# Moving a cluster step between two matmul stages of an attention kernel, and loading the first q by contiguous rows

## The chip, the core and the metric

The kernel runs on one core of one Trainium2 chip. The metric is the device time of one execution in microseconds (us), the median of the runs of a kernel. The core has five engines that run their own instruction queues side by side and meet only through semaphores: TensorE (PE in the profile, its weight loads PEld), VectorE (DVE), ScalarE (ACT), GpSimd (POOL) and SyncE (SP, here only an issuer of DMAs).

## What is computed

A routing attention is followed by a mixture of experts. Each query and each key is assigned to the most similar of 16 cluster centroids of its head, and a query attends only to keys of its own cluster.

```python
# B, H, S, D = 4, 8, 768, 64; 16 clusters
q_assign = np.argmax(np.einsum('bhsd,hcd->bhsc', q_n, c_n), axis=-1)
k_assign = np.argmax(np.einsum('bhsd,hcd->bhsc', k_n, c_n), axis=-1)
mask = q_assign[:, :, :, None] == k_assign[:, :, None, :]
scores = np.where(mask, scale * np.matmul(q, k.transpose(0, 1, 3, 2)), -1e9)
attn = softmax(scores)
attn_out = np.matmul(attn, v)
# x = attn_out as (3072, 512): each token goes to the best of 8 experts (512 -> 1024 -> 512, relu)
```

## The kernel before

The attention works through 16 pairs of heads (NG = 16; a pair is two heads of one batch, and fills the 128 partitions). The order of instructions on each engine is the order of the program. A pair is a **turn**: twelve units of scores, then the jobs of the part "mid", then twelve units of weighted values, then the jobs of the part "end".

```python
for n in range(-4, NTURN + 2):
    for i, x in enumerate(range(n * NB, (n + 1) * NB)):     # NB = 12
        if 0 <= x < NU:
            score(x)
        run(n, i)
    run(n, mid)
    for i, x in enumerate(range(n * NB, (n + 1) * NB)):
        if 0 <= x < NU:
            attend(x)
        run(n, NB + i)
    run(n, end)
```

One unit of scores: four fp32 matmuls in two halves of the array's rows and two bf16 ones that add the cluster mask (`ohT`), an exponential on ScalarE, and a sum over key blocks on VectorE. The first block of a half has no sum of its own, so twelve units make ten sums.

```python
def score(u):
    ps = ps_s.tile([P, 2, 512], F32, name="sps")            # 3 buffers
    # ... matmul(ps, lhsT=qk[g], rhs=qk[g]) x2, matmul(ps, lhsT=ohT[g], rhs=ohT[g]) x2
    A[u] = ap.tile([P, 2, HS], F32, name="A")
    nc.scalar.activation(A[u], ps[:, :, 0:HS], AF.Exp, scale=D**-0.5)      # line 1005
    if g == NG - 2 and u % UG >= 3:                         # UG = 12
        later_sums.append((u, A[u]))
    else:
        add_up(u, A[u])                                     # DVE: lines 1019 and 1023
```

The cluster step of a pair makes `ohT` for its scores: similarities on TensorE, the maximum and its place on VectorE, one product on GpSimd, a transposition, and eight copies on ScalarE.

```python
def similar(g):
    ps = ps_o.tile([P, 512], F32, name="O") if g == 1 else wide()[:, 0, :]   # wide(): one of the 3 "sps"
    # ... 4 matmuls, each in its own quarter of the array's columns (line 914)
    sims[g] = asg.tile([P, HS], F32, name="sim")
    nc.vector.transpose(sims[g], ps[:, 0:HS])               # line 921

def assign(g):
    nc.vector.tensor_reduce(mx, sim, axis=AX, op=ALU.max)                    # line 930
    nc.vector.tensor_tensor(sim, sim, mx..., op=ALU.is_ge)                   # line 931
    (nc.gpsimd if g > 1 else nc.vector).tensor_tensor(sim, sim, first_c..., op=ALU.mult)   # line 932

def assign2(g):
    nc.vector.tensor_reduce(top, rank, axis=AX, op=ALU.max)                  # line 939
    nc.vector.tensor_tensor(oh, rank, top..., op=ALU.is_equal)               # line 941
    nc.vector.transpose(sims[g], oh)                        # "ohs", line 946

def put_by_scalar(g):
    # 4 times: copy (line 960) and activation (line 961) from ohs into ohT[g]
```

`weigh` sums the weights (12 fp32 matmuls, line 1060, also in quarters of the array's columns) and its result is transposed on VectorE (line 1068). `turn_blocks` transposes q and k of a pair on VectorE (line 899, two instructions). `finish` copies the output of a half on ScalarE (line 1046), `keep` transposes it on VectorE (line 1089) and stores it by DMAs from GpSimd. The jobs are placed so:

```python
for f in (similar, assign, assign2):
    at(0, 4, f, 1)
for g in range(NG):
    at(g, end, finish, g, 0)
    at(g, end, finish, g, 1)
    if g + 2 < NG:
        at(g, mid, turn_blocks, g + 2)
        at(g, end, similar, g + 2)
        at(g, end, assign, g + 2)
    if g < NG - 1:
        at(g, end, keep, g, 0, S)
        at(g + 1, mid, weigh, g)
        at(g, mid, put_by_scalar, g + 1)
    if g + 2 < NG:
        at(g, end, assign2, g + 2)
```

So the cluster step of a pair runs at the end of the turn two before its own, and its copies into `ohT` run in the middle of the next turn. For the first pair alone q and k are transposed by TensorE instead of VectorE (`turn`), because they are loaded whole:

```python
(nc.scalar if g == 0 and name == "k" else nc.sync).dma_start(       # line 775
    out=t[:, :, a, :],
    in_=src[b, 2 * hp + a].rearrange("(j p) d -> p j d" if name == "q" else "(p j) d -> p j d", j=NQ),
)
```

Of the kernel before, what the change touches and what calls it, by code (L numbers as in the profile page):

```python
# [8 lines left out]
F32 = mybir.dt.float32  # L9
# [176 lines left out]
def kernel(  # L186
# [11 lines left out]
    nc = tc.nc  # L198
    B, H, S, D = q.shape
    C = centroids.shape[1]  # L200
    P = 128
    NQ = S // P
# [3 lines left out]
    NG = B * HP  # L206
# [27 lines left out]
    def fetch1(e, i):  # L234
        w1 = wpool.tile([P, DB, F], F32, name=f"w1_{i % 2}")
        nc.sync.dma_start(out=w1, in_=moe_w1[bass.ds(e, 1)].rearrange("e (a p) f -> p (e a) f", p=P))
        return w1
# [29 lines left out]
    ps_o = late.enter_context(tc.tile_pool(name="ps_o", bufs=2, space=PSUM))  # L267
# [3 lines left out]
    def apart(first, second):  # L271

        first, second = (getattr(i, "ins", i) for i in (first, second))
        tc.declare_no_dep(second, first, reason="other banks and other elements")


    def wide():
        return pools["s"].tile([P, 2, 512], F32, name="sps")
# [4 lines left out]
    def bank():  # L283

        return wide()[:, 0, :] if "attention" in pools else ps_o.tile([P, 512], F32, name="O")
# [450 lines left out]
    with ExitStack() as actx:  # L736
# [17 lines left out]
        def load_qk(g):  # L754
            b, hp = divmod(g, HP)
            for name, src in (("q", q), ("k", k)):
                t = rows[g, name] = ld.tile([P, NQ, 2, D], F32, name=name + "_in")
                for quad in range(4 if g else 0):


                    a, d0 = quad // 2, quad % 2 * 32
                    o = t[quad * 32 : (quad + 1) * 32].rearrange("p j a d -> p (j a d)")
                    if name == "q":
                        nc.sync.dma_start(  # L764
                            out=o.rearrange("p (b d) -> p b d", d=32),
                            in_=src[b, 2 * hp + a].rearrange("(b p) d -> p b d", p=32)[:, :, d0 : d0 + 32],
                        )
                    else:
                        nc.sync.dma_start(
                            out=o.rearrange("p (i m d) -> p i m d", m=4, d=32),  # L770
                            in_=src[b, 2 * hp + a].rearrange("(m p i) d -> p i m d", m=4, i=NQ)[:, :, :, d0 : d0 + 32],
                        )
                for a in range(0 if g else 2):

                    (nc.scalar if g == 0 and name == "k" else nc.sync).dma_start(
                        out=t[:, :, a, :],
                        in_=src[b, 2 * hp + a].rearrange("(j p) d -> p j d" if name == "q" else "(p j) d -> p j d", j=NQ),
                    )

        def load_v(g):  # L780
# [35 lines left out]
        ps = bank()  # L816
# [44 lines left out]
        def blocks():  # L861
            cps = bank()
            nc.tensor.transpose(cps[:, 0:P], cn.rearrange("p a d -> p (a d)"), ident)
            cview = cps[:, 0:P].rearrange("p (g a c) -> p g a c", a=2, c=C)
            for a in range(2):
                nc.vector.tensor_copy(cblk[a * D : (a + 1) * D, :, a, :], cview[a * D : (a + 1) * D, :, a, :])


        qk, sims, ohT = {}, {}, {}

        def turn(g, piece):

            if piece == 0:
                qk[g] = qkp.tile([P, 2, S], F32, name="qk")
            n = NQ - 4 if piece else 4
            ps = wide().rearrange("p a c -> p (a c)")
            for i in range(2 * n):
                w, j = divmod(i, n)
                if i == n and piece == 0:
                    blocks()  # L880
                nc.tensor.transpose(
                    ps[:, w * 512 + j * P : w * 512 + (j + 1) * P], rows[g, "qk"[w]][:, 4 * piece + j].rearrange("p a d -> p (a d)"), ident
                )
            if piece == 0:
                apart(
                    nc.vector.tensor_copy(qk[g][:, 0, 0:512], ps[:, 0:512]),
                    nc.scalar.copy(qk[g][:, 1, 0:512], ps[:, 512:1024]),
                )
            else:
                apart(*(  # L890
                    copy(qk[g][:, w, 512:S], ps[:, w * 512 : w * 512 + n * P])
                    for w, copy in enumerate((nc.vector.tensor_copy, nc.scalar.copy))
                ))

        def turn_blocks(g):

# [10 lines left out]

        def similar(g):


            ps = ps_o.tile([P, 512], F32, name="O") if g == 1 else wide()[:, 0, :]
            for t in range(4):
                w, half = divmod(t, 2)
                nc.tensor.matmul(  # L914
                    ps[t * 2 * C : (t + 1) * 2 * C, 0:HS], lhsT=cblk[:, g % HP].rearrange("p a c -> p (a c)"),
                    rhs=qk[g][:, w, half * HS : (half + 1) * HS], start=True, stop=True,
                )


            sims[g] = asg.tile([P, HS], F32, name="sim")  # L920
            nc.vector.transpose(sims[g], ps[:, 0:HS])
# [64 lines left out]
        A, T, O = {}, {}, {}  # L986
        XT = {}

        def where(u):
            g, r = divmod(u, 2 * NQ)  # L990
            return g, r // NQ, r % NQ

        def score(u):
            g, half, j = where(u)
            qs = slice(half * HS, (half + 1) * HS)
            ks = slice(j * P, (j + 1) * P)
            ps = ps_s.tile([P, 2, 512], F32, name="sps")
            for a in range(2):
                r = slice(a * D, (a + 1) * D)
                nc.tensor.matmul(ps[:, a, 0:HS], lhsT=qk[g][r, 1, ks], rhs=qk[g][r, 0, qs], start=True, stop=False)  # L1000
            for a in range(2):
                r = slice(a * D, (a + 1) * D)
                nc.tensor.matmul(ps[:, a, 0:HS], lhsT=ohT[g][r, 1, ks], rhs=ohT[g][r, 0, qs], start=False, stop=True)  # L1003
            A[u] = ap.tile([P, 2, HS], F32, name="A")
            nc.scalar.activation(A[u], ps[:, :, 0:HS], AF.Exp, scale=D**-0.5)  # L1005
            if g == NG - 2 and u % UG >= 3:
                later_sums.append((u, A[u]))
            else:
                add_up(u, A[u])
# [3 lines left out]
        def add_up(u, a_u):  # L1013
            g, half, j = where(u)
            if j == 0:
                last_a[0] = a_u
            elif j == 1:
                T[g, half] = tp_.tile([P, 2, HS], F32, name="T", bufs=4)
                nc.vector.scalar_tensor_tensor(
                    T[g, half], in0=last_a[0], scalar=1e-9 / P, in1=a_u, op0=ALU.add, op1=ALU.add  # L1020
                )
            else:
                nc.vector.tensor_tensor(T[g, half], T[g, half], a_u, op=ALU.add)  # L1023
# [110 lines left out]
        def at(n, part, f, *a):  # L1134
            jobs.setdefault((n, part), []).append((f, a))

        UG = 2 * NQ
# [3 lines left out]
        mid, end = "mid", "end"  # L1141
# [9 lines left out]
        at(0, 2, put_q, 0, 1)  # L1151
        at(-2, end, idle_of, 20)
        at(-1, end, turn_blocks, 1)
        for f in (similar, assign, assign2):
            at(0, 4, f, 1)
        for g in range(NG):
            at(g, end, finish, g, 0)
            at(g, end, finish, g, 1)
            if g + 2 < NG:
                at(g, mid, turn_blocks, g + 2)  # L1160
                at(g, end, similar, g + 2)
                at(g, end, assign, g + 2)
            if g < NG - 1:
                at(g, end, keep, g, 0, S)
                at(g + 1, mid, weigh, g)
                at(g, mid, put_by_scalar, g + 1)
            if g + 2 < NG:
                at(g, end, assign2, g + 2)
            if g % HP == HP - 1 and g < NG - 1:
                at(g + 1, mid, gate, g // HP)  # L1170
                at(g + 1, end, gate2, g // HP)
                at(g + 1, end, keep_pads, g // HP)
# [44 lines left out]
        n = NG - HP  # L1217
# [4 lines left out]
        at(n + 1, end, one_hots1, 1)  # L1222

        at(n + 2, UG + 3, tokens1)
        at(n + 2, UG + 3, sums_of_later, 2)
        at(n + 2, UG + 6, spread1)
        at(n + 2, UG + 6, gather1, 0)
        at(n + 2, UG + 6, sums_of_later, UG)
        at(n + 3, mid, gather1, 1)
        at(n + 3, mid, turn_rows1, 0)  # L1230

        n = NG
# [54 lines left out]
    with tc.tile_pool(name="sm", bufs=1) as sm:  # L1287
# [20 lines left out]
        for part in parts:  # L1308
            n, over = part["n"], part["over"]
# [95 lines left out]
    g = groups[0]  # L1405
# [61 lines left out]
    with tc.If(more > 0):  # L1467
        nx = nc.values_load(xe[0:1, NX : NX + 1], min_val=0, max_val=NX)
        general = nc.values_load(xe[0:1, NX + 1 : NX + 2], min_val=0, max_val=1)
        with tc.If(nx > XU):  # L1470
            with ExitStack() as ectx:
# [3 lines left out]
                with tc.For_i(XU, nx, 1) as i:  # L1475
# [5 lines left out]
                    g = dict(  # L1481
                        n=[P], rows=N, w=(fetch1(ex, 0), fetch2(ex, 0)), gi=lambda j, i: gi[:, i : i + 1],
                        si=lambda j: gi[:, 4:5], apart=False,
                    )
# [37 lines left out]
```

## Time and profile before

| what | value |
|---|---|
| median of 3 runs | 687.94 us (687.89 to 688.46) |
| span of the profiled execution | 687.2 us |
| TensorE busy | 674.8 us, 98% of the span |
| VectorE busy | 471.8 us, 69% |
| ScalarE busy | 310.6 us, 45% |
| GpSimd busy | 253.6 us, 37% |
| first exponential of pair 1, of pair 15 | 37.12 us, 313.73 us |
| last attention output copied | 331.6 us |

The first 332 us are the attention, the rest is the mixture of experts, which the change leaves as it is. The share of busy time is an average over both; the attention has to be read turn by turn. A busy TensorE is not TensorE at its peak, since the ends of pipelined matmuls are modelled. A timeline line gives start, length, engine, source line, operation, what it writes and reads, the number of instructions merged into it, and in brackets the idle time before it with what ended it.

### The profile page before, as it was taken

The page shows a single profiled execution, that of the slowest core. Times are in us where ns is not written, and L with a number is a line of the kernel's source. Part 1 is how long each engine was busy: PE and PEld are TensorE (multiplying, and loading weights), DVE is VectorE, ACT ScalarE, POOL GpSimd, SP SyncE. Part 2 cuts the span into 40 slices and gives each one's busy share as a digit, 9 for nine tenths or more (in the row PEclk, how much of TensorE's full clock was granted, in tenths as well). Part 3 has the DMA queues.
Part 4 walks back from the last instruction along what each step waited for, and adds up shares of the span by engine and source line. Part 5 has one row for each costly group of instructions (what it writes and reads, how often), then busy time and mean ns, then how long its engine had stood idle before and what let it go on. Part 6 is the DMA issues. An engine that isn't in the chain of part 4 may idle for free.

```text
span 687.2 us, 11979 instructions
## 1 busy us (share of the span) xinstructions
PE 674.8 (98%) x4603; PEld 440.1 (64%) x4603; DVE 471.8 (69%) x740; ACT 310.6 (45%) x470; POOL 253.6 (37%) x327
## 2 busy tenths in 40 slices
PE   8999999999999999999999999999999999999994
PEld 7444444445454444555656789878788787888761
DVE  6887888779887778889666549576755767564300
ACT  3887777778877777785111031211113111131100
POOL 5022222122222221257816774547352563412101
PEclk9999999999999999999999999999999999999997
DMA  7566864997759643421435349586676866668440
GB/s 144 90 93 93 154 140 86 152 150 153 117 74 195 98 68 38 49 48 33 68 125 176 119 135 371 198 291 207 233 268 212 306 195 236 244 230 300 161 140 20
DMA packets 149540, 106.71 MB, mean 155 GB/s; under 512 B 115554, under 2 KB 119650, under 8 KB 149475
## 3 DMA queue, kind: packets, MB, share of 16 engines
q1 hardware_dynamic: 135266, 77.41, 42.9%
q0 software_dynamic: 8640, 19.63, 13.0%
q10 hardware_dynamic: 5568, 8.83, 4.3%
q8 instruction: 38, 0.62, 0.4%
q14 instruction: 28, 0.22, 0.1%
HBM read 93.06 MB, written 13.30 MB: 155 GB/s over the span
## 4 chain that ended last, share of the span: by engine, by line
PE 74%; issue 14%; POOL 6%; DVE 2%; DMA 1%; SPq 1%; POOLq 0%; ACTq 0%; ACT 0%; DVEq 0%
PE sps L1000 17%; PE O L1038 17%; PE sps L321 9%; PE sps L498 8%; PE sps L386 7%; PE sps L520 5%; PE sps L1003 4%; POOL xg L292 3%; PE sps L1060 3%; POOL out_dram L341 2%; PE sps L914 2%; DMA k_in<-in_k_dram 1%; PE sps L357 1%; DVE T L1023 1%; SPq L764 0%
## 5 line engine op out<-in xcount | busy, mean ns | idle before, releaser
L1005 ACT ACTIVATE A<-sps 128x768 f32<-128x768 f32 x192 | 153.7, 810 | 22.3 <-PE sps L1003 21.0
L292 POOL DMA_INDIRECT xg<-x_rows,g_idx x104 | 120.4, 1158 | 115.5 <-DVE xgT L308 81.1
L1000 PE MATMUL sps<-qk 64*128 64x384 f32 x768 | 157.0, 487 | 0.0
L1023 DVE TENSOR_TENSOR T<-T,A 128x768 f32<-128x768 f32 x128 | 122.6, 958 | 13.1
L1038 PE MATMUL O<-A,v_in 128*64 128x384 f32 x768 | 127.8, 488 | 0.0
L1000 PEld LDWEIGHTS sps<-qk 64*128 64x128 f32 x768 | 67.6, 187 | 48.7 <-issue 44.5
L1038 PEld LDWEIGHTS O<-A,v_in 128*64 128x64 f32 x768 | 53.6, 137 | 67.0 <-issue 65.0
L1003 PE MATMUL sps<-ohT 64*128 64x384 bf16 x384 | 63.6, 322 | 0.0
L386 PE MATMUL sps<-w,h_sb 128*128 128x512 f32 x144 | 63.1, 592 | 0.0
L341 POOL DMA_INDIRECT out_dram<-zo,s_idx x32 | 37.5, 1172 | 67.6 <-ACT zo L337 25.1
L321 PEld LDWEIGHTS sps<-xgT,w 128*128 128x128 f32 x448 | 51.0, 192 | 3.7 <-issue 3.7
L321 PE MATMUL sps<-xgT,w 128*128 128x128 f32 x448 | 51.3, 275 | 0.0
L1072 POOL COPY dens<-ls 128x12 f32<-128x12 f32 x16 | 3.6, 226 | 124.3 <-DVE ls L1068 124.3
L1091 POOL DMA_DIRECT2D x_rows<-xb x68 | 48.3, 718 | 2.1 <-issue 0.7
L932 POOL TENSOR_TENSOR sim<-sim,first_c 128x384 f32<-128x384 f32 x14 | 14.0, 1002 | 91.2 <-DVE sim L931 91.2
L386 PEld LDWEIGHTS sps<-w,h_sb 128*128 128x128 f32 x144 | 26.8, 190 | 30.6 <-issue 30.6
L961 ACT ACTIVATE ohT<-ohs,big 32x384 bf16<-32x384 bf16 x60 | 42.0, 700 | 0.8
L364 ACT COPY zc<-sps 32x512 f32<-32x512 f32 x24 | 13.9, 578 | 60.2 <-PE sps L357 60.0
L337 ACT COPY zo<-sps 128x512 f32<-128x512 f32 x12 | 7.0, 586 | 71.3 <-PE sps L386 65.5
L498 PEld LDWEIGHTS sps<-xs,w1s 128*128 128x128 f32 x288 | 36.0, 190 | 5.0 <-DVE xs L409 4.2
L498 PE MATMUL sps<-xs,w1s 128*128 128x144 f32 x288 | 37.9, 288 | 0.0
L331 ACT ACTIVATE h_sb<-sps 128x512 f32<-128x512 f32 (+1 forms) x18 | 9.6, 578 | 58.1 <-PE sps L321 58.1
(265 smaller groups left out, 953.3 us busy)
## 6 DMA issues: line engine op xcount, KB each, us to landing
w<-in_moe_w_dram SPq DMA_DIRECT2D x28, 2048.0 KB, 9.3
w<-in_moe_w_dram ACTq DMA_DIRECT2D x16, 512.0 KB, 4.5
v_in<-in_v_dram SPq DMA_DIRECT2D x16, 384.0 KB, 3.5
q_in<-in_q_dram SPq DMA_DIRECT2D x60, 96.0 KB, 4.0
k_in<-in_k_dram SPq DMA_DIRECT2D x60, 96.0 KB, 5.2
x_rows<-xb POOLq DMA_DIRECT2D x60, 96.0 KB, 5.3
xg<-x_rows,g_idx POOLq DMA_INDIRECT x104, 3.3
x_rows<-pad SPq DMA_DIRECT2D x64, 3.0 KB, 2.6
```

The lines of the kernel that those rows point to most:

```text
L292: nc.gpsimd.indirect_dma_start(out=g["xg"][:, n, :], out_offset=None, in_=x_q[0 : 4 * g["rows"], :], in_offset=bass.IndirectOffsetOnAxis(a ...
L321: nc.tensor.matmul(o, lhsT=g["w"][0][:, c, fb * P : (fb + 1) * P], rhs=g["xT"][:, c, :cols], start=(c == 0), stop=(c == DB - 1),)
L341: ins = nc.gpsimd.indirect_dma_start(out=out[:, :], out_offset=bass.IndirectOffsetOnAxis(ap=g["si"](j)[0:m], axis=0), in_=zo[0:m], in_offs ...
L386: nc.tensor.matmul(zp, lhsT=g["h"][:, fb, j * P : (j + 1) * P], rhs=g["w"][1][:, fb, :], start=(fb == 0), stop=(fb == FB - 1),)
L498: nc.tensor.matmul(o, lhsT=a[:, c, f * P : (f + 1) * P], rhs=b[:, c, :], start=(c == 0), stop=(c == KH - 1),)
L961: nc.scalar.activation(ohT[g][r, 1, cols], t[k], AF.Identity, scale=big[k, a, 0:1], bias=big[k, a, 1:2])
L1000: nc.tensor.matmul(ps[:, a, 0:HS], lhsT=qk[g][r, 1, ks], rhs=qk[g][r, 0, qs], start=True, stop=False)
L1003: nc.tensor.matmul(ps[:, a, 0:HS], lhsT=ohT[g][r, 1, ks], rhs=ohT[g][r, 0, qs], start=False, stop=True)
L1005: nc.scalar.activation(A[u], ps[:, :, 0:HS], AF.Exp, scale=D**-0.5)
L1023: nc.vector.tensor_tensor(T[g, half], T[g, half], a_u, op=ALU.add)
L1038: nc.tensor.matmul(O[g, half][a * D : (a + 1) * D, 0:HS], lhsT=rows[g, "v"][:, a, j, :], rhs=a_[:, a, :], start=(j == 0), stop=(j == NQ - 1),)
L1091: nc.gpsimd.dma_start(out=x_d[b * S + c0 : b * S + c1, quad, hp * 32 : (hp + 1) * 32].rearrange("(n t) d -> t n d", t=32), in_=xb[quad * 3 ...
```

## The change

The cluster step of the next pair moves from the end of the turn before to the middle of the present turn, where its matmuls stand directly ahead of those of `weigh`. The purpose is that two stages which use the array in the same way (quarters of its columns) stand together, so that TensorE changes its way of working once less in a turn, and that the special first case at unit 4 goes away. So that VectorE reaches the cluster step sooner, the sums of the last two units of a turn wait: one is done between `assign` and `assign2`, one after it. The copies of `put_by_scalar` follow in the same place. In the last turn but one, where nine sums already waited, two of the nine are done there, and the places of two later jobs move by two units. Besides, q of the first pair is loaded with each partition's six rows contiguous in memory, and the copies out of PSUM put the columns back in order with a step of six elements.

```diff
-                        in_=src[b, 2 * hp + a].rearrange("(j p) d -> p j d" if name == "q" else "(p j) d -> p j d", j=NQ),
+                        in_=src[b, 2 * hp + a].rearrange("(p j) d -> p j d", j=NQ),
 ... (in turn, the first pair)
+            q_cols = qk[g][:, 0, :].rearrange("d (p j) -> d j p", j=NQ)[:, 4 * piece : 4 * piece + n, :]
-                    nc.vector.tensor_copy(qk[g][:, 0, 0:512], ps[:, 0:512]),
+                    nc.vector.tensor_copy(q_cols, ps[:, 0:512].rearrange("d (j p) -> d j p", p=P)),
 ... (the same for the second piece)
-            ps = ps_o.tile([P, 512], F32, name="O") if g == 1 else wide()[:, 0, :]
+            ps = wide()[:, 0, :]
 ... (in score)
-            if g == NG - 2 and u % UG >= 3:
+            if g < NG - 1 and u % UG >= (3 if g == NG - 2 else UG - 2):
                 later_sums.append((u, A[u]))
 ... (the jobs)
-        for f in (similar, assign, assign2):
-            at(0, 4, f, 1)
         for g in range(NG):
             at(g, end, finish, g, 0)
             at(g, end, finish, g, 1)
+            if g < NG - 1:
+                at(g, mid, similar, g + 1)
+                at(g, mid, assign, g + 1)
+                at(g, mid, sums_of_later, 1)
+                at(g, mid, assign2, g + 1)
+                at(g, mid, sums_of_later, 1)
+                at(g, mid, put_by_scalar, g + 1)
+            if g > 0:
+                at(g, mid, weigh, g - 1)
             if g + 2 < NG:
                 at(g, mid, turn_blocks, g + 2)
-                at(g, end, similar, g + 2)
-                at(g, end, assign, g + 2)
             if g < NG - 1:
                 at(g, end, keep, g, 0, S)
-                at(g + 1, mid, weigh, g)
-                at(g, mid, put_by_scalar, g + 1)
-            if g + 2 < NG:
-                at(g, end, assign2, g + 2)
+        for g in range(NG):
 ... (gate as before)
-        at(n + 2, UG + 3, sums_of_later, 2)
-        at(n + 2, UG + 6, spread1)
-        at(n + 2, UG + 6, gather1, 0)
-        at(n + 2, UG + 6, sums_of_later, UG)
+        at(n + 2, UG + 8, spread1)
+        at(n + 2, UG + 8, gather1, 0)
+        at(n + 2, UG + 8, sums_of_later, UG)
```

More of the change, by code (lines that the diff above doesn't have):

```diff
@@ L889, in turn @@
             else:
[L890 to L893, printed above, removed]
+                apart(
+                    nc.vector.tensor_copy(q_cols, ps[:, 0 : n * P].rearrange("d (j p) -> d j p", p=P)),
+                    nc.scalar.copy(qk[g][:, 1, 512:S], ps[:, 512 : 512 + n * P]),
+                )
         def turn_blocks(g):
```

## The prediction, made before the changed kernel was run

> **What bounds the kernel now.** I read the engine table first, then the busy times by stage, then the chain of waits over one turn, then the timelines of ScalarE and VectorE through the same kind of turn.
>
> Engine table of the page:
>
> ```profile
> PE 674.8 (98%) x4603; PEld 440.1 (64%) x4603; DVE 471.8 (69%) x740; ACT 310.6 (45%) x470; POOL 253.6 (37%) x327
> ```
>
> Busy times by stage; the line is pairs 1 to 13 (us, then PE, PEld, DVE, ACT, POOL, clock, DMA share, GB/s):
>
> ```profile
> 37.00:292.90 255.90, 255.90 (x1978) 125.50 (x1976) 213.47 (x310) 200.27 (x289) 63.92 (x113) 1.00 0.66 110
> ```
>
> TensorE has no idle time in this stage and its full clock; VectorE is at 83%, ScalarE at 78%. The chain of waits over one turn (start, length, what) stays on TensorE:
>
> ```profile
> 124.75 1.11 PE sps L1060 x24
> 125.86 7.89 PE O L1038 x48
> 133.75 0.78 PE sps L914 x8
> 134.53 0.85 PE sps L1000 x4
> ```
>
> From one line 1060 to the next a turn takes 19.67 us (66.69 to 86.36 for line 1038): twelve scores at 0.81, weigh 1.11, values 7.89, similarities 0.78. A pair of fp32 matmuls of 384 columns otherwise takes 0.65, so 0.13 of the similarities and 0.20 of the first score (0.85) look like the price of changing stage.
>
> ScalarE through one turn (the second and third copy pairs are cut):
>
> ```profile
> 56.73 9.69 ACT L1005 ACTIVATE A<-sps 128x768 f32<-128x768 f32 x12 [1.30 <-PE sps L1003]
> 66.45 0.51 ACT L960 COPY ohT<-ohs 32x384 bf16<-32x384 bf16 x1
> 66.97 0.70 ACT L961 ACTIVATE ohT<-ohs,big 32x384 bf16<-32x384 bf16 x1
> ...
> 71.43 0.48 ACT L1046 COPY xT<-O 128x384 f32<-128x384 f32 x1
> 74.63 0.48 ACT L1046 COPY xT<-O 128x384 f32<-128x384 f32 x1 [2.72 <-PE O L1038]
> 76.41 9.70 ACT L1005 ACTIVATE A<-sps 128x768 f32<-128x768 f32 x12 [1.30 <-PE sps L1003]
> ```
>
> The reader should see two things. The eight copies into the mask follow the exponentials with no gap: their input has been ready for long. And ScalarE's idle time, 2.72 + 1.30 = 4.02 us a turn, all lies after the copies.
>
> VectorE through the same turn:
>
> ```profile
> 55.75 0.58 DVE L921 STREAM_TRANSPOSE sim<-sps 128x384 f32<-128x384 f32 x1 [2.50 <-PE sps L914]
> 56.37 0.55 DVE L930 TENSOR_REDUCE mx<-sim 128x24 f32<-128x384 f32 x1
> 56.96 0.56 DVE L931 TENSOR_TENSOR sim<-sim,mx 128x384 f32<-128x384 f32 x1
> 57.43 0.97 DVE L1089 STREAM_TRANSPOSE xb<-xT 128x768 f32<-128x768 f32 x1
> 58.62 0.55 DVE L939 TENSOR_REDUCE top<-sim 128x24 f32<-128x384 f32 x1 [0.22 <-POOL sim L932]
> 59.21 0.56 DVE L941 TENSOR_TENSOR oh<-sim,top 128x384 bf16<-128x384 f32 x1
> 59.81 0.58 DVE L946 STREAM_TRANSPOSE ohs<-oh 128x384 bf16<-128x384 bf16 x1
> 60.31 0.92 DVE L1019 SCALAR_TENSOR_TENSOR T<-A 128x768 f32<-128x768 f32 x1
> ...
> 70.51 0.38 DVE L1068 STREAM_TRANSPOSE ls<-sps 128x192 f32<-128x192 f32 x1
> ```
>
> The cluster step is hidden at the start of a turn, while the first exponentials run; from the first transposition to the end of the last it takes 60.39 - 55.75 = 4.64 us. Then ten sums take 10.20 us, 1.02 each, slower than the 0.81 us of an exponential. Here the sums are 4 us behind at mid, and nobody waits for them.
>
> **What the Trainium skill says.** "PSUM — Partial Sum Buffer", "Engine vs sequencer instructions": the queues of ScalarE, VectorE and GpSimd are strictly first in, first out. The trace agrees: the copies, then the output copies, then the exponentials, in program order. So whatever delays the mask copies delays the next turn's exponentials.
>
> "SBUF — State Buffer", "Who interferes with whom": a VectorE instruction with two SBUF inputs and a GpSimd instruction that reads SBUF exclude each other; the later one waits for the whole of the first. The trace agrees where both meet:
>
> ```profile
> 329.21 1.52 POOL L1075 TENSOR_TENSOR lgh<-ls,rd 128x96 f32<-128x96 f32 x1
> ```
>
> The same instruction has a median of 0.355 us; here VectorE's two-input product of line 305 ran from 329.00 to 330.51.
>
> "TensorE: Matmul & The Clock Gate", "What's actually happening": the clock falls after about 3.4 us idle. No idle that I expect is that long, so I count no loss of clock; the trace before has no such idle in this stage and doesn't test it.
>
> **The change part by part.** Let e be the start of the first exponential of a turn, and follow everything to the same event of the next.
>
> 1. *TensorE.* One change of stage less: 0.13 to 0.2 us a turn, over 14 turns about 2 to 3 us if TensorE stays the bound. Its own work is then some 19.5 us a turn.
>
> 2. *VectorE up to the cluster step.* Eight of ten sums now stand ahead of it. The first needs the second exponential: e + 0.80 + 0.81 + 0.07 = e + 1.68 (0.80 is ScalarE's pace when it has a backlog, 7.17 us for nine in turn 0). keep's transposition ends by e + 1.05 and doesn't delay it. Eight sums at 1.017 (60.31 to 65.39 is five): e + 9.82. The similarities are out of TensorE by about e + 9.56 (the last score ends at e + 8.8, plus 0.78), so VectorE decides.
>
> 3. *The cluster step.* 4.64 us as before gives e + 14.46. But the tenth sum now stands where keep's one-input transposition stood, beside GpSimd's product (line 932, 1.00 us in each of its 14 runs). The sum has two SBUF inputs, so by the lock above one waits for the other, whichever is first: product and sum come to 2.0 us instead of 1.1, and the maximum after them needs both. That adds 0.9: e + 15.36.
>
> 4. *ScalarE.* The copies start 0.09 later (27.40 to 27.49 in turn 0), take 4.98 (66.45 to 71.43), and the two output copies 0.49 each: e + 15.36 + 0.09 + 4.98 + 0.98 = **e + 21.4**. This is a closed loop of ScalarE and VectorE: exponentials, eight sums, cluster step, copies, exponentials. TensorE can run ahead only by the three score buffers. With 19.5 of its own it waits some 1.9 us a turn, and the period goes from 19.67 to 21.4, by 1.75 us. Without the lock's 0.9 it is 20.5, by 0.85.
>
> 5. *Single turns.* Turn 0: VectorE's transpositions of pair 1 end at 19.24 (k lands at 18.2), eight sums end at 27.4, the cluster step with one sum in it and the product on VectorE takes 5.15, copies and outputs 6.0, so pair 1's first exponential is at 38.6 instead of 37.12. Turns 1 to 12: 12 x 21.4, plus 0.5 for the three turns with a softmax of the gate on ScalarE, 257.3. Turn 13: five instructions of line 632 to 640 (1.8 us) now stand ahead of its sums and delay all, 23.2. Turn 14: only two sums stand ahead, the similarities decide, 21.2. Sum: 38.6 + 257.3 + 23.2 + 21.2 = 340.3 for pair 15's first exponential, against 313.73: **26.6 us more**.
>
> 6. *The rest.* The seven sums left over for turn 15 and the later gathers: about half a microsecond. The first q: k lands at 6.70 and TensorE's warm-up matmuls end near 7.3, so an earlier q hides behind both; the first similarities now need both pieces of q. I count 0 to 0.4 us lost.
>
> Sum: 687.9 + 26.6 + 0.5 = 715. Without the lock: 15 x 0.85, the extra of turns 0 and 13, about 15 more, 703. I give the lock three chances in four: **712 us**.
>
> **Rivals.**
> - *TensorE stays the bound* and gains the change of stage: 685 to 686. For it: TensorE is busy throughout and ScalarE and VectorE have 20% to spare. Against it: the spare time lies after the copies, and the new order puts 4.8 to 5.7 us of waiting ahead of them.
> - *The lock doesn't bite* (GpSimd's product and the sum overlap): 703.
> - *The loop is partly hidden*, since three score buffers let TensorE run ahead: against it, a head start is spent once and the loop recurs fifteen times. It would make 695 to 700.
> - *Issues of weight loads on ScalarE's queue* (two a turn in turns 2 to 9) fall after the copies and lengthen the loop. Mostly they took 0.8 us beside the copies, but in one turn they held the output copy by 1.36 us: up to 718.
>
> **Range and chances.** The range covers the loop with and without the lock, and 0.3 us error a turn: 700 to 720. 2% slower is 701.7, which only the rivals and the lower edge of the no-lock case stay under: slower 0.84, same 0.14, faster 0.02.
>
> **What would show it.** In the changed profile TensorE has idle time in each turn, ended by ScalarE; line 960 waits some 5 us for ohs of line 946 after the exponentials; the output copies and exponentials follow with no gap; a turn takes 21.4 us; line 932 lasts near 2 us, or line 1023 beside it does. A period of 20.5 with a 1.0 us product refutes the lock; a period under 19.7 refutes the loop. The prediction fails if the copies do not stand ahead of the output copies and exponentials on ScalarE, or if the sums run faster than 1.0 us.

## The result and the profile after

The changed kernel takes 707.05 us (median of 6 runs, 706.03 to 708.01) against 688.23 us for the kernel before: 2.7% slower, ratio 1.0271 with a 95% interval of 1.0256 to 1.0285. The prediction was 712 us with a range of 700 to 720.

All of it arises in the attention. Pair 15's first exponential comes at 332.51 us instead of 313.73, 18.8 us later, and from there to the end both kernels take the same (705.8 - 332.51 = 373.3 us, before 687.2 - 313.73 = 373.5 us). Turns are counted here from one pair's first exponential to the next pair's: turn 1 starts with pair 1's.

Engine table and chain of the page after, and as the last line the chain of the page before:

```profile
PE 676.4 (96%) x4603; PEld 440.3 (62%) x4603; DVE 470.6 (67%) x740; ACT 303.3 (43%) x470; POOL 262.4 (37%) x327
...
PE 41%; ACT 20%; issue 16%; DVE 11%; POOL 8%; DMA 1%; ACTq 1%; POOLq 0%; DVEq 0%
...
PE 74%; issue 14%; POOL 6%; DVE 2%; DMA 1%; SPq 1%; POOLq 0%; ACTq 0%; ACT 0%; DVEq 0%
```

No compute engine but GpSimd became appreciably busier, so no work of weight was added; but ScalarE and VectorE now hold 31% of the chain that ends last, against 2% before. Busy times of one turn, from one pair's first exponential to the next (us, PE, PEld, DVE, ACT, POOL, clock, DMA share, GB/s):

```profile
58.63:79.35 20.72, 19.81 (x152) 9.68 (x152) 15.87 (x21) 14.85 (x24) 5.63 (x9) 1.00 0.60 104
```

A turn takes 20.72 us and TensorE, without a gap before, is idle for 0.91 of it: it makes three scores of the next pair ahead, one for each score buffer, and waits at the fourth until ScalarE has worked off the first:

```profile
59.51 0.92 PE L1001 MATMUL sps<-qk 64*128 64x384 f32 x4 [0.91 <-ACT A L1006]
```

ScalarE through this turn:

```profile
58.63 9.27 ACT L1006 ACTIVATE A<-sps 128x768 f32<-128x768 f32 x12
73.63 0.51 ACT L961 COPY ohT<-ohs 32x384 bf16<-32x384 bf16 x1 [5.73 <-DVE ohs L947]
74.15 0.70 ACT L962 ACTIVATE ohT<-ohs,big 32x384 bf16<-32x384 bf16 x1
...
78.60 0.86 ACT L1047 COPY xT<-O 128x384 f32<-128x384 f32 x2
79.35 9.27 ACT L1006 ACTIVATE A<-sps 128x768 f32<-128x768 f32 x12
```

The idle time has changed its place: 5.73 us ahead of the mask copies, waiting for the cluster step, and none after them. Copies, outputs and the next exponentials follow head to tail. VectorE and GpSimd in the same turn (two timelines):

```profile
60.20 0.96 DVE L1020 SCALAR_TENSOR_TENSOR T<-A 128x768 f32<-128x768 f32 x1 [0.44 <-ACT A L1006]
...
68.32 0.58 DVE L922 STREAM_TRANSPOSE sim<-sps 128x384 f32<-128x384 f32 x1
...
69.99 0.95 DVE L1024 TENSOR_TENSOR T<-T,A 128x768 f32<-128x768 f32 x1
71.83 0.55 DVE L940 TENSOR_REDUCE top<-sim 128x24 f32<-128x384 f32 x1 [0.89 <-POOL sim L933]
...
73.01 0.58 DVE L947 STREAM_TRANSPOSE ohs<-oh 128x384 bf16<-128x384 bf16 x1
```

```profile
70.15 1.65 POOL L933 TENSOR_TENSOR sim<-sim,first_c 128x384 f32<-128x384 f32 x1 [7.25 <-DVE sim L932]
```

Eight sums stand from 60.20 to 68.32, then the cluster step. Its product on GpSimd, 1.00 us before, takes 1.65 beside a sum, and VectorE waits 0.89 us for it. That holds for all 14 products (before, then after: count, then shortest, median and longest ns, first and last start):

```profile
L932 POOL TENSOR_TENSOR sim<-sim,first_c x14: 997/1002/1012, 37.9 to 294.7; 128x384 f32<-128x384 f32 x14
L933 POOL TENSOR_TENSOR sim<-sim,first_c x14: 1638/1648/1652, 49.4 to 323.3; 128x384 f32<-128x384 f32 x14
```

In the list of waits over the whole run (us in total, times, longest), that of the mask copies for the cluster step and that of TensorE for the exponentials:

```profile
ACT ohT L961 <- DVE ohs L947: 87.1, 15, 7.6
PE sps L1001 <- ACT A L1006: 16.6, 15, 2.1
```

### The profile page after: what moved, and what is told of

Read it like the earlier page. It is cut to its first block, busy times and chain, and to the rows that moved or that the text cites. A ratio compares the mean times of both kernels' runs of the same rounds, so it can differ in the third digit from the quotient of the medians.

```text
span 705.8 us, 11952 instructions
## 1 busy us (share of the span) xinstructions
PE 676.4 (96%) x4603; PEld 440.3 (62%) x4603; DVE 470.6 (67%) x740; ACT 303.3 (43%) x470; POOL 262.4 (37%) x327
## 4 chain that ended last, share of the span: by engine, by line
PE 41%; ACT 20%; issue 16%; DVE 11%; POOL 8%; DMA 1%; ACTq 1%; POOLq 0%; DVEq 0%
ACT A L1006 11%; PE sps L321 9%; PE sps L498 8%; PE sps L386 7%; PE sps L520 5%; PE O L1039 5%; PE sps L1001 4%; ACT ohT L962 4%; DVE T L1024 4%; ACT ohT L961 3%; POOL xg L292 3%; POOL sim L933 3%; POOL out_dram L341 2%; ACT xT L1047 2%; PE sps L357 1%
## 5 line engine op out<-in xcount | busy, mean ns | idle before, releaser
L1001 PE MATMUL sps<-qk 64*128 64x384 f32 x768 | 160.2, 495 | 16.6 <-ACT A L1006 16.6
L1006 ACT ACTIVATE A<-sps 128x768 f32<-128x768 f32 x192 | 148.8, 817 | 2.2 <-PE sps L1004 1.8
L961 ACT COPY ohT<-ohs 32x384 bf16<-32x384 bf16 x60 | 30.6, 510 | 88.0 <-DVE ohs L947 87.1
L933 POOL TENSOR_TENSOR sim<-sim,first_c 128x384 f32<-128x384 f32 x14 | 23.1, 1647 | 100.3 <-DVE sim L932 100.3
L1090 DVE STREAM_TRANSPOSE xb<-xT 128x768 f32<-128x768 f32 (+1 forms) x17 | 15.8, 930 | 38.9 <-ACT xT L1047 36.4
```

The lines of the kernel that those rows point to most:

```text
L961: nc.scalar.copy(ohT[g][r, 0, cols], t[i])
```

## The experiments

The theory: a closed loop of exponentials, eight sums, cluster step, mask copies, output copies and the next exponentials is longer than TensorE's own work in a turn; and part of its length is the exclusion of a two-input VectorE instruction and a GpSimd instruction. The rivals: the loads of the first q, a worse place for the similarities on TensorE, a product that is slow for another reason.

### The load alone

```diff
 (kernel before)
+  in_=src[b, 2 * hp + a].rearrange("(p j) d -> p j d", j=NQ)     # for q too
+  nc.vector.tensor_copy(q_cols, ...)                             # columns with a step of six
```

> The kernel before with only the first q loaded by contiguous rows. In the changed kernel the first scores start 0.35 us earlier (14.72 against 15.07 us) and pair 1's loads too. The loop theory says that the loads are no part of the slowdown: 687.5 to 688.2 us, the same as before within 0.1%. A rival in which the first q carries part of the loss would show up to several us more.

Measured: 688.75 us, ratio 1.0009 (1.0001 to 1.0017), 0.5 us above the expected range. The load has next to no part in the slowdown of 18.8 us, and it brings nothing. The copies with a step took back what it gave (VectorE by line and shape: count, busy time, mean ns, idle before):

```profile
L887 DVE COPY qk<-sps 128x512 f32<-128x512 f32 x1 | 1.1, 1065 | 0.0
L892 DVE COPY qk<-sps 128x256 f32<-128x256 f32 x1 | 0.6, 598 | 0.0
```

Before, the same two took 690 and 410 ns. ScalarE's copy of k began 0.53 us earlier (7.89 against 8.42), the two q copies are 0.56 us longer together, and the first exponential starts at 16.40 against 16.35. (Pair 1's comes 0.58 us earlier in this trace, since VectorE had no wait for pair 1's k. The load is not shown to be the reason: in the changed kernel, with the same load, VectorE waited 0.86 us for it, in the kernel before 0.82.)

### Both sums behind the cluster step

```diff
-                at(g, mid, sums_of_later, 1)
                 at(g, mid, assign2, g + 1)
-                at(g, mid, sums_of_later, 1)
+                at(g, mid, sums_of_later, 2)
                 at(g, mid, put_by_scalar, g + 1)
```

> The changed kernel with both waiting sums behind the whole cluster step, so that nothing with two SBUF inputs runs on VectorE beside GpSimd's product. If the two exclude each other (lock theory): the product falls from 1.65 to 1.00 us, the maximum after it starts 0.64 us earlier, and each of 14 turns is 0.64 us shorter: 20.1 us a turn, 698 us in all. If they don't and the product is slow for another reason, or if the sum fitted into the wait: no change, 707 us.

Measured: 698.51 us, ratio 1.0158 (1.0141 to 1.0174). GpSimd and ScalarE in one turn (two timelines):

```profile
68.98 1.00 POOL L933 TENSOR_TENSOR sim<-sim,first_c 128x384 f32<-128x384 f32 x1 [7.24 <-DVE sim L932]
```

```profile
71.81 0.51 ACT L961 COPY ohT<-ohs 32x384 bf16<-32x384 bf16 x1 [5.07 <-DVE ohs L947]
```

The product is back at 1.00 us (14 runs, 0.994 to 1.004), the wait of the copies falls by 0.66 us, and a turn takes 20.07 us (57.47 to 77.54). VectorE is faster here with nothing to do while it waits: the sum that was put into this wait of 1.11 us lengthened the loop by 0.65 us.

### No sum waiting

```diff
-            if g < NG - 1 and u % UG >= (3 if g == NG - 2 else UG - 2):
+            if g == NG - 2 and u % UG >= 3:
```

> The changed kernel with no sum waiting: all ten sums stand ahead of the cluster step (the last turn but one keeps its nine). Loop theory: VectorE reaches the cluster step 2 x 1.015 us later and loses the 0.64 us of the product beside a sum, so a turn takes 20.72 + 2.03 - 0.64 = 22.1 us, and 13 turns add 18 us: 725 us. If the loss came from TensorE (a worse place for the similarities) or from the copies' number alone, it stays at 707 us or falls, since no work is added.

Measured: 733.0 us, ratio 1.0641 (1.0625 to 1.0657). No work was added, and the kernel is 26 us slower than the changed one: so the loop through VectorE's sums sets the time. Several turns took 22.2 us (62.65 to 84.85), as expected. The 8 us beyond the expectation are mostly in five turns of 23.3 to 23.6 us, and come from TensorE's clock. First TensorE's timeline at the start of such a turn, then the busy times of three stretches of 3.41 us around it (last columns clock, DMA share, GB/s):

```profile
85.73 1.65 PE L1001 MATMUL sps<-qk 64*128 64x384 f32 x4 [2.13 <-ACT A L1006]
87.49 1.49 PE L1001 MATMUL sps<-qk 64*128 64x384 f32 x4
```

```profile
82.35:85.75 3.40, 1.27 (x12) 0.60 (x8) 0.75 (x1) 3.35 (x7) 0.00 (x0) 1.00 1.01 331
85.76:89.17 3.41, 3.41 (x14) 1.84 (x16) 2.66 (x4) 2.13 (x3) 2.86 (x4) 0.50 1.32 232
89.18:92.58 3.40, 3.40 (x28) 1.97 (x26) 2.34 (x3) 3.18 (x4) 0.00 (x0) 1.00 1.25 113
```

After 2.13 us without work the granted clock was 0.50, and groups of four matmul instructions that otherwise span 0.81 us (0.92 for the first of a turn) took 1.5 to 1.65; 3.41 us later the clock was back. The trace has fourteen waits of 1.8 us and more at the start of a turn. The four of 1.82 to 1.84 us left the clock alone; seven of the ten of 2.05 to 2.38 us did not.

The trace also shows why three of the ten did no harm. The seven low stretches of these turns last 3.41 us each and begin at 41.38, 85.76, 154.03, 222.29, 290.56, 314.45 and 338.34 us, that is 13, 20, 20, 20, 7 and 7 times 3.41 us apart. So in this trace the clock is decided on a grid of 3.41 us, to which the kernel's own turns have no fixed place. Each of the seven waits lies within one cell of this grid, and the next cell has the low clock. The other three are cut by an edge of the grid, with at most 1.36 us in one cell; one of them (129.11 to 131.49 us), the longest of all with 2.38 us:

```profile
126.72:130.13 3.41, 2.39 (x18) 1.11 (x13) 0.49 (x3) 3.32 (x7) 0.00 (x0) 1.00 0.69 244
130.13:133.54 3.41, 2.05 (x15) 1.22 (x17) 2.83 (x8) 3.39 (x7) 1.75 (x3) 1.00 0.31 88
```

In this trace 1.83 us without work in one cell left the clock at 1.00, and 2.05 us halved it.

### The copies split between two engines

```diff
 (put_by_scalar)
-                    nc.scalar.activation(ohT[g][r, 1, cols], t[k], AF.Identity, scale=..., bias=...)
+                    nc.vector.tensor_scalar(ohT[g][r, 1, cols], t[k], scalar1=..., scalar2=..., op0=ALU.mult, op1=ALU.add)
 (the jobs: put_by_scalar ahead of the second waiting sum)
```

> The changed kernel with the four mask copies of k on VectorE (ahead of the second waiting sum), four of q left on ScalarE. Loop theory: ScalarE's part of the loop falls from 4.97 to 2.05 us and the loop to about 17.8 us, below TensorE's own 19.5 us; TensorE is the bound again and a turn takes 19.5 to 19.7 us: 685 to 690 us. VectorE then has about 19.6 us of work and waits in a turn and may itself be the bound, up to 692 us. If the loss came from the similarities' place on TensorE: still about 707 us.

Measured: 694.95 us, ratio 1.0096 (1.0081 to 1.0111). The loop is broken in the plain turns; busy times of one:

```profile
74.63:94.17 19.54, 19.54 (x154) 9.72 (x152) 17.36 (x26) 12.63 (x19) 5.63 (x9) 1.00 0.75 134
```

TensorE is without a gap again and a turn takes 19.54 us, 0.13 less than before the change: that is what the change of stage was worth. Twelve scores take 9.89 us and the values 7.89 in both; the similarities take 0.67 us (83.38 to 84.05) instead of 0.78, and the sums of weights 1.09 instead of 1.11. The total misses the expectation by 5 us. TensorE's waits say where: 1.65 us at the start of turn 5, 2.04 at the start of turn 6, 1.03 and 0.93 in turn 14, and 0.65 at the start of the experts.

Turns 4 and 14 (21.9 and 23.2 us) ran out of time on VectorE, which has more to do there and four copies more at 0.39 us. In turn 4 ScalarE waits 2.29 us for VectorE's part of the gate's softmax, which its next exponentials stand behind. Turn 5 (21.8 us) is not VectorE's: ScalarE's output copies, whose input was complete at 134.10, stood behind two issues of weight loads on its own queue:

```profile
135.00 2.04 ACTq L1258 DMA_DIRECT2D w<-in_moe_w_dram  x2
137.13 0.86 ACT L1047 COPY xT<-O 128x384 f32<-128x384 f32 x2 [3.96 <-PE sps L1004]
```

Turns 8 and 12 took 20.5 us from exponential to exponential, but TensorE lost no more than 0.29 us after each: the score buffers absorb a single late turn.

### Filling the gap with a one-input instruction

```diff
 (on top of the copies split)
-                at(g, mid, sums_of_later, 1)
+                at(g, mid, turn_block, g + 2, 0)      # the transposition of the next q, moved from turn_blocks
                 at(g, mid, assign2, g + 1)
                 at(g, mid, put_by_scalar, g + 1)
-                at(g, mid, sums_of_later, 1)
+                at(g, mid, sums_of_later, 2)
```

> The changed kernel with the four k copies on VectorE, the transposition of the next q (one SBUF input) beside GpSimd's product instead of a sum, and both waiting sums behind the copies. Lock theory: the product beside a one-input instruction lasts 1.00 us, not 1.65, and VectorE gains some 0.9 us a turn against the run with the copies split, so that it has about 18.5 us of work in TensorE's 19.54. Loop theory: 19.54 us a turn, and the turns that stuck on VectorE there (21.9, 21.8, 20.5, 20.5, 23.2 us) come down by about 1 us each: 687 to 691 us. If the product stays at 1.65 us, the lock is not about two inputs, and the time stays at 695 us.

Measured: 692.38 us, ratio 1.0059 (1.0045 to 1.0073). The product's line (count, then shortest, median and longest ns, first and last start):

```profile
L939 POOL TENSOR_TENSOR sim<-sim,first_c x14: 1000/1004/1009, 47.8 to 306.1; 128x384 f32<-128x384 f32 x14
```

A transposition of 0.97 us in the very place of a sum of 0.95 us leaves the product at 1.00: it is not the company of any VectorE instruction that delays it. The second input explains the difference; a one-input instruction other than this transposition was not tried. The time is 1.4 us above the expected range: TensorE still waits 1.18 us after turn 4 (21.4 us), 0.93 and 1.36 us in turn 14 (23.6 us) and 0.68 at the start of the experts.

### Fewer copies on VectorE, and the last turns

```diff
 (in put_by_scalar)
+                    if half == 0:      # only the first half's k copies on VectorE
```

> The same with only the two k copies of the first half on VectorE, the other two on ScalarE. By the measured parts the loop is 1.57 + 8.12 + 4.64 + 0.04 + 3.5 + 0.75 = 18.6 us, still below TensorE's 19.54, and VectorE has 0.75 us less, about 17.8 us. Loop theory: 19.54 us a turn, and the turns with extra work on VectorE gain up to 0.75 us each: 686 to 689 us, at best level with or 0.2% below the kernel before. If the bound of those turns is ScalarE, it is slower than the run with all four on VectorE.

Measured: 688.4 us, ratio 1.0000 (0.9992 to 1.0009): level with the kernel before. Up to turn 12 it gains (pair 13's first exponential comes at 270.94 us against 273.65), the last turns lose most of it (pair 15's: 312.44 against 313.73). Busy times of turn 13, and TensorE where it starts on the experts:

```profile
271.00:291.40 20.40, 20.40 (x162) 10.25 (x156) 18.92 (x34) 13.39 (x21) 4.70 (x8) 1.00 0.38 46
```

```profile
332.02 1.21 PE L321 MATMUL sps<-xu,w 128*128 128x288 f32 x4 [0.65 <-DVE xu L308]
```

VectorE is busy for 18.92 of 20.40 us there, with almost no wait between its instructions. But TensorE is busy for the whole 20.40 us; it waits for VectorE only afterwards, 0.73 us in turn 14 and 0.65 at the start of the experts. Two attempts to take work off VectorE in these turns followed.

```diff
 (first attempt)
-                    if half == 0:
+                    if half == 0 and g < NG - 2:                      # no copies of turns 13, 14 on VectorE
-            (nc.gpsimd if g > 1 else nc.vector).tensor_tensor(        # the product of turn 14 on VectorE
+            (nc.gpsimd if 1 < g < NG - 1 else nc.vector).tensor_tensor(
-                at(g, mid, sums_of_later, 2)
+                if g < NG - 2:                                        # no sums in the middle of turn 14
+                    at(g, mid, sums_of_later, 2)
```

> The run with two k copies on VectorE, with less on VectorE in the last two turns that have a cluster step, where it was without idle time: all mask copies of turns 13 and 14 on ScalarE (2 x 0.77 us off VectorE), the product of turn 14 on VectorE (0.56 us instead of 1.11 us of waiting for GpSimd), and the nine sums of turn 14 all left for later. If VectorE is the bound from turn 13 to the end of the attention, the experts' first rows are turned some 2 us earlier, TensorE's wait of 0.65 us for them goes: 686 to 687.5 us, 0.1 to 0.3% below the kernel before. If TensorE or ScalarE bounds these turns: 688.4 us, no change.

Measured: 690.87 us, ratio 1.0044 (1.0032 to 1.0056), a miss. TensorE's wait grew, and VectorE's timeline shows why:

```profile
333.92 1.45 PE L321 MATMUL sps<-xu,w 128*128 128x288 f32 x5 [2.00 <-DVE xu L308]
```

```profile
292.97 0.98 DVE L1101 STREAM_TRANSPOSE xb<-xT 128x768 f32<-128x768 f32 x1 [2.10 <-ACT xT L1058]
```

With all copies of turn 13 on ScalarE the loop is back in that turn, its end is 1.4 us later (292.82 against 291.43), and VectorE sits idle for 2.10 us; with all sums of turn 14 left for later it idles another 1.66 us ahead of the row numbers. It was relieved and made to wait. The second attempt leaves turn 13 and the sums alone:

```diff
-                    if half == 0:
+                    if half == 0 and g < NG - 1:                      # no copies of turn 14 on VectorE
 (the product of turn 14 on VectorE, as above)
```

> As the run with two k copies on VectorE, but in turn 14 alone all mask copies are on ScalarE and the product is on VectorE; the sums stay where they were, and turn 13 is untouched. That takes 0.77 us of copies and some 0.55 us of waiting off VectorE in a turn where it was without idle time, without lengthening the loop of turn 13 as the run before this one did. If VectorE bounds the last turns: TensorE's waits of 0.73 and 0.65 us there shrink, 687 to 688 us. If the loop through ScalarE's copies bounds turn 14 too: 688.4 us or more.

Measured: 0.9976 of the kernel before (0.9961 to 0.9991). This run was on another chip, where the kernel before took 701.47 us and this one 700.22, so only the ratio is read. The extra time of that chip lies behind the attention: from the experts' first matmul to the end this run takes 368.3 us, the run with two k copies 354.6. TensorE now goes over to the experts without a wait, and 1.82 us earlier than in the trace of the kernel before (this run, then the kernel before):

```profile
330.80 1.45 PE L321 MATMUL sps<-xu,w 128*128 128x288 f32 x5
...
332.62 3.66 PE L321 MATMUL sps<-xu,w 128*128 128x288 f32 x14
```

This version keeps the similarities beside the sums of weights, as the change wanted, and beats the kernel before by 0.24%, measured on that one chip. Against the changed kernel it is some 3% faster by an estimate from the two ratios (0.9976 and 1.0271).

## Why the prediction was right, and where its sizes were off

*The loop* (steps 2 to 4) is as predicted: the signs named for it are in the trace (with a product of 1.65 us for one near 2), and each run that lengthened or shortened one member of it moved the turn as its sum said. The size was 21.4 us against 20.72 measured. The terms, from exponential to exponential in us:

| term | predicted | measured | why |
|---|---|---|---|
| to the first sum | 1.68 | 1.57 | twelve exponentials in a row take 9.27, 0.77 each, not 0.80 |
| eight sums | 8.14 | 8.12 | |
| cluster step with the lock | 5.54 | 5.27 | the lock adds 0.63, not 0.9 |
| to the copies | 0.09 | 0.04 | |
| eight copies | 4.98 | 4.97 | |
| two output copies | 0.98 | 0.75 | back to back they overlap, 0.86 for both to their end |
| turn | 21.41 | 20.72 | |

The term that was most mis-sized is step 3's "product and sum come to 2.0 us instead of 1.1". They came to 1.8: the product ended at 71.80, 0.86 us after the sum's end at 70.94, not a whole 1.00. The other two errors are alike: durations of instructions that had waited for something were taken for durations in a queue without waits. So the nine exponentials of turn 0 (7.17 us) had no backlog in the kernel before: TensorE's scores for them came every 0.81 us. In the changed kernel the same nine take 6.83 us. All three errors make the loop shorter than predicted.

That 712 us came so close is partly luck. It was weighed from 715 with the lock and 703 without it, and 707 lies between the two, so the total alone doesn't tell them apart. Nor does the turn: 20.72 us is nearer to the 20.5 named for no lock than to 21.4. What tells is the product of 1.65 us, and that it is 1.00 us without the sum. With the lock, pair 15's first exponential was predicted at 340.3 us and came at 332.5; turns 1 to 12 make 7.3 us of this difference (250.0 us against 257.3).

*The lock* (three chances in four) is shown by two runs: take the sum away, or put a one-input transposition in its place, and the product is 1.00 us again. The prediction's 703 us for a kernel without it was some 5 us high, for the same small terms: without a sum beside the product the kernel took 698.5.

*TensorE stays the bound* fell: 0.91 us of idle time in each turn. The gain that it promised is real, 0.13 us a turn, and shows as soon as the loop is out of the way. *The loop is partly hidden* fell too: TensorE is three scores ahead in every turn and still waits 0.91 us. What the buffers hide is a single late turn, as turns 8 and 12 of the run with the copies split. *Issues of weight loads on ScalarE's queue* cost nothing in most turns: in the turn quoted they were issued at 75.41 between the copies. In turn 5 they held the output copies, by 0.40 us in the changed kernel, 1.21 us with both sums behind the cluster step and some 3 us with the copies split.

*Single turns*: turn 0 ended at 37.91, predicted 38.6, and turn 13 took 22.6, predicted 23.2. Turn 14 took 22.0, predicted 21.2: its clock was 0.92, after a wait of 2.13 us. The 2.13 us lie within one cell of the clock's grid (308.66 to 312.07), and the clock was 0.50 in the next. There the step "I count no loss of clock" failed; it holds for the plain turns, whose waits were 0.91 us at a clock of 1.00.

*The first q*: 0 to 0.4 us lost was predicted; the load alone cost 0.5 us, and the interval of its ratio (1.0001 to 1.0017) just excludes none.

What stays open: whether the stage change costs the same in other orders (only this one was tried), what held the issues of weight loads in turn 5, and whether the gain of 0.24% is the same on other chips.

## What to carry to other kernels

An engine's idle time is worth only what stands behind it: before, ScalarE's four idle microseconds lay after its copies, where they could absorb a delay; a job that hands it its input later moves the idle time ahead of the copies and closes a loop, though no work is added. Before moving a producer closer to its consumer, follow one event around to its next occurrence over all engines, with durations from stretches without waits, and compare that sum with the bound engine's own time. And when filling a gap on VectorE beside a GpSimd instruction that reads SBUF, fill it with a one-input instruction, as here with a transposition.

## What was not expected of the hardware

- TensorE's granted clock fell to 0.50 for 3.41 us after waits of 2.05 to 2.38 us that lay within one cell of a grid of 3.41 us, and not after waits as long that an edge of the grid cut. The prediction leaned on "TensorE: Matmul & The Clock Gate", "What's actually happening", of the Trainium skill, which lets the clock fall after an idle window of about 3.4 us and calls the window free-running. The grid agrees with that; but 2.05 us without work in a window were enough here, and there the measurement decides.
- Copies from PSUM with a step of six elements in what they write took 1.06 us for 512 columns instead of 0.69, and 0.60 for 256 instead of 0.41.
- A GpSimd product that is shut out by a VectorE sum ended 0.86 us after the sum, though alone it lasts 1.00 us.
